# A new plan for the first part of a three-stage kernel, a lag in one group's output products, and an order edge for late diagonals

## The chip, the cores and the metric

The kernel runs on one core of one Trainium2 chip. The metric is the device time of one execution in microseconds (us). Six engines' work is told apart in the profile: PE (matrix products) and PEld (its weight loads), DVE, ACT and POOL (element-wise work), and SP, which issues most of the transfers.

## The reference

Three stages follow one another on 3072 tokens (4 sequences of 768) of 384 numbers (8 heads of 48):

```
state = 0                                  # per sequence and head, 48 x 48
for t: y[t] = r[t] @ (state + (u*k[t]) v[t]^T)
       state = w * state + k[t] v[t]^T
x   = (sigmoid(y @ w_gate) * (y @ w_val)) @ w_out       # 384 -> 1536 -> 384
e   = argmax of normalised x against 8 expert vectors; gate = its softmax share
out = gate * (relu(x @ w1[e]) @ w2[e])                  # 384 -> 1024 -> 384
```

## The kernel before, in words

**Tiling.** The tokens are 24 chunks of 128 (`c` = 0 to 23; six chunks make a sequence, each with its own state) and 12 groups of two chunks (`g` = 0 to 11). A chunk goes through: load; scaling of r and k by powers of w (`at_p`, or L911 to L914 for chunks 0 to 3); the row sums of r*k*u (`at_sd`, L548, DVE); the diagonal blocks built from them (`at_diag`, ACT L563 for the first heads, POOL L558 for the rest); the score products (`native_A`, L576, PE) and their masking into the same tile (`native_mask`, L585, DVE); products with v (`at_P` L599, `at_Y1` L619, PE), the state update (`at_T`, L610 to L615, DVE), products with the state (`at_Y2`, L619, PE), the copy of the result into the operand `xt` (`at_X`, L669 to L674, ACT and DVE), and, for every second chunk from 4 on, six small transfers on POOL's queue that put 16 rows of each half of `xt` in place (`at_D`, L682). From chunk 9 on, all of `at_p` is on POOL (L536 to L540); before that its large part is on DVE (L534). `load_chunk(c + 3)` (L352, SP) is called with `at_X(c)`, since the new chunk takes the buffer of chunk c.

**The gated product** of a group has 12 blocks. `emit_gv` makes 18 PE products for one block (`pgv`, L698) and then the gate: sigmoid on ACT (L725), the product on DVE (L727), a rounded copy on ACT (L729), and the remainder on DVE (L730, called lo here). `emit_out` adds the block to the output with 6 PE products (`o`, L741). Groups 0 and 1 are done one by one with `emit_gv`; groups 2 to 11 are done in pairs by `emit_wide` with 512 columns (`pgate`, `pval`, L698; sigmoid L707, product L711, copy L713, lo L715).

**The weights** of the gated product come as 64-bit words and are converted in 18 units (12 `gv`, 6 `wo`): a copy on ACT (L403), three DVE operations (L405 to L407), a copy on ACT (L413 or L421), and a remainder on DVE (L415 or L430); `wo` units also need PE transposes (L427) and products with the normalised expert vectors (L438), which `embeddings` makes (L482 to L494: ACT, a change of ACT's table for a square root, six tiny DVE operations, one of 8x384, three PE transposes, a copy).

**What sets the order.** In the first part (chunks 0 to 8, groups 0 and 1, the 18 units) each job is a generator with due times (`CHUNK_AT`, `CHUNK_T`, `LATE_T`, `CONV_AT`, `CONV_T`, `GV_AT`, `GV_T`, ...). A loop takes, again and again, the job with the smallest due time whose need is met and issues its next piece; a piece that had to wait shifts the rest of its job. The due times are only a numbering: nothing waits for a clock. The instructions that this loop issues until the due time passes `IN_ORDER` are tied to one another engine by engine (`in_order`). The order in which the rest is issued is a priority; the framework's scheduler sets the final order of each engine and may put an instruction that is ready ahead of earlier ones. An explicit `follow(a, b)` puts a behind b on its engine without a wait across engines. After the first part, `steps` runs the wide groups: a step is one block f of a pair and two ticks, and the pieces of chunks 9 to 23 are attached to ticks.

At chunk c of the wide part the row sums come in the tick before the masks:

```
if st == -2: at_p(c)
elif st == 1: at_s1(c)          # at_sd, then at_diag
elif st == 2: native_mask(...)
elif st == 4: at_P(c); at_Y1(c); at_T(c)
```

Of the kernel before, what the change touches and what calls it, by code (L numbers as in the profile page):

```python
# [15 lines left out]
ALU = mybir.AluOpType  # L16
AX = mybir.AxisListType
# [7 lines left out]
REGION = 480  # L25
FIRST = 3 * ST
W_MIN, W_MAX = 0.6, 1.5
ACT_HEADS = (8, 4, 8, 8, 3, 2)
PERM = 4
HALF = 64  # L30
HEADS = ((0, 2), (4, 6), (3, 1), (7, 5))
# [7 lines left out]
INIT_AT = (85.0, 2.0)  # L39
INIT_AFTER = 14  # L40
AT_ROWS = 5
CONV_T = (1.67, 3.44, 4.6, 6.42, 8.97)
CHUNK_T = ((7.0, 7.63, 8.6, 8.7, 8.8, 9.77, 12.24, 12.24, 12.3, 13.2, 15.5, 15.6), (10.2, 10.25, 10.4, 12.7, 15.28, 16.78, 18.77, 19.4, 19.5, 20.2, 22.47, 22.47), (1.2, 2.51, 3.71, 4.31, 4.51, 4.51, 8.19, 8.19, 8.2, 8.3, 9.34, 9.34), (1.2, 2.51, 3.71, 4.31, 4.51, 4.51, 7.36, 7.4, 7.42, 7.5, 9.34, 9.51))
LATE_T = {-2: 0, 0: 0.1, 1: 6.1, 2: 5.5, 3: 12.0, 5: 11.9}
CHUNK_AT = (0.0, 0.0, 20.0, 28.97, 70.45, 69.16, 92.51, 111.47, 151.21)
CONV_AT = (12.48, 16.92, 18.32, 4.98)
IN_ORDER = 15.4
EMB_AT = 14.6
NUMBERS_AT = 60.0
WARM = 12  # L50
WARMS = ((8.37, 4), (10.35, 3), (23.91, 0), (23.04, 2))
GV_T = (4.82, 5.87, 8.45)
GV_AT = (10.27, 43.91)


@with_exitstack
def kernel(
# [14 lines left out]
    nc = tc.nc  # L72
# [6 lines left out]
    NF = 12  # L79
# [29 lines left out]
    def follow(ins, before):  # L109

        tc.add_manual_dep(
            ins, before.name,
            mybir.DependencyInfo(mybir.DependencyClass.NoSync, mybir.DependencyReason.DATA), reason="order",
        )
# [9 lines left out]
    def wtile(nm):  # L124
        return wp.tile([P, 1568], F32R, tag="w", name=nm)
# [170 lines left out]
    if True:  # L296
# [76 lines left out]
        wo = {}  # L373
# [19 lines left out]
        def words(n, dt):  # L393
            return slot[n].bitcast(dt).rearrange("p (n t) -> p n t", t=2)

        def conv(n):
# [6 lines left out]
            nc.scalar.activation(x, words(n, F32)[:, :, 1], AF.Abs, scale=2.0 ** -112)  # L403
            yield CONV_T[0], None
            nc.vector.tensor_scalar(xi, xi, 3, None, op0=ALU.logical_shift_left)  # L405
            nc.vector.scalar_tensor_tensor(xi, w[:, :, 1], -2147483648, xi, op0=ALU.bitwise_and, op1=ALU.bitwise_or)  # L406
            nc.vector.scalar_tensor_tensor(xi, w[:, :, 0], 29, xi, op0=ALU.logical_shift_right, op1=ALU.bitwise_or)  # L407
            slot.pop(n)
            yield CONV_T[2], None
            w = wtile(kind)  # L410
            lo = nc.gpsimd if n in POOL_LO else nc.vector
            if kind == "gv":
                nc.scalar.activation(w[:, 0:768], x, AF.Copy)  # L413
                yield CONV_T[3], None
                lo.tensor_tensor(w[:, 768:1536], x, w[:, 0:768], op=ALU.subtract)  # L415
# [5 lines left out]
            nc.scalar.activation(wv[:, :, 0, 0:384], xv, AF.Copy)  # L421
            yield CONV_T[2], ("x", 1)
            xT = tmpp.tile([P, 2, 3, P], F32, tag="x", name="xT")
            for f in range(2):
# [3 lines left out]
                nc.scalar.activation(xT[:, f], pt, AF.Copy)  # L428
            yield CONV_T[3], None
            lo.tensor_tensor(wv[:, :, 1, 0:384], xv, wv[:, :, 0, 0:384], op=ALU.subtract)  # L430
            avail["x"] += 1
            yield CONV_T[4], "en"

# [67 lines left out]
        sd = [sds[:, 0], sds[:, 1]]  # L501
# [17 lines left out]
        def fields(t):  # L519
            rT = t[:, 0:512].rearrange("p (a n) -> p a n", a=4)  # L520
            kT = t[:, 512:1024].rearrange("p (a n) -> p a n", a=4)
            kt = t[:, 1024:1408].rearrange("p (h d) -> p h d", h=8)
            v = t[:, 1408:1920].rearrange("p (h d) -> p h d", h=8)
            r = t[:, 1920:2304].rearrange("p (h d) -> p h d", h=8)
            return rT, kT, kt, v, r
# [16 lines left out]
        def at_s1(c):  # L542
            at_sd(c)
            at_diag(c)

        def at_sd(c):
            rT, kT, kt, v, r = fields(ld[c])
            nc.vector.tensor_reduce(sd[c % 2], r, axis=AX.X, op=ALU.add)  # L548

        def at_diag(c):  # L550
            if c < 4 and c % 2 == 1:
# [3 lines left out]
            ams[c] = Am  # L555
            n = ACT_HEADS[c] if c < len(ACT_HEADS) else 0
            if n < 8:
# [126 lines left out]
                        )  # L684

        gts = {}
        po = {}
        open_y = []
        scores = {}

        def gate_half(pg, s, f, x):
            w = gvw[f]
            n = 0
            for k in range(3):
                o = s * 384 + k * P
                wh, wl = w[:, o:o + P], w[:, 768 + o:768 + o + P]
                for a, b in ((wh, 0), (wh, 1), (wl, 0)):
                    nc.tensor.matmul(pg, a, x[:, k, b, :], start=(n == 0), stop=(n == 8))  # L698
                    n += 1

        def emit_wide(g, f):

            x = xt[g // 2]
            p0 = ps_gv.tile([P, 512], F32, tag="gv", name="pgate")
            gate_half(p0, 0, f, x)
            sg = tmpp.tile([P, 512], F32, tag="x", name="sgw")
            nc.scalar.activation(sg, p0, AF.Sigmoid)  # L707
            yield
            p1 = ps_gv.tile([P, 512], F32, tag="gv", name="pval")
            gate_half(p1, 1, f, x)  # L710
            nc.vector.tensor_tensor(sg, p1, sg, op=ALU.mult)  # L711
            hi = gtp.tile([P, 512], F32R, tag="gt", name="gth")
            nc.scalar.activation(hi, sg, AF.Copy)  # L713
            lo = gtp.tile([P, 512], F32R, tag="gt", name="gtl")
            nc.vector.tensor_tensor(lo, sg, hi, op=ALU.subtract)  # L715
            for i in range(2):
                gts[g + i, f] = [t[:, i * 256:(i + 1) * 256] for t in (hi, lo)]

        def emit_gv(g, f):
            x = xt[g // 2][:, :, :, (g % 2) * 256:(g % 2) * 256 + 256]  # L720
            pg = ps_gv.tile([P, 2, 256], F32, tag="gv", name="pgv")
            for s in range(2):
                gate_half(pg[:, s, :], s, f, x)
            sg = sgp.tile([P, 256], F32, tag="sg", name="sg")
            nc.scalar.activation(sg, pg[:, 0, :], AF.Sigmoid)  # L725
            gf = sg
            nc.vector.tensor_tensor(gf, pg[:, 1, :], sg, op=ALU.mult)  # L727
            gt = gtp.tile([P, 2, 256], F32R, tag="gt", name="gt")
            nc.scalar.activation(gt[:, 0, :], gf, AF.Copy)  # L729
            nc.vector.tensor_tensor(gt[:, 1, :], gf, gt[:, 0, :], op=ALU.subtract)  # L730
            gts[g, f] = [gt[:, i] for i in range(2)]

        def emit_out(g, f):
            gt = gts.pop((g, f))
            w = wo[f // 2]
            if f == 0:
                po[g] = [ps_o.tile([P, 392], F32, tag=f"o{g % 2}{t}", name=f"o{t}") for t in range(2)]
            for t in range(2):
                ts_ = slice(t * P, (t + 1) * P)
                for n, (a, b) in enumerate(((0, 0), (0, 1), (1, 0))):  # L740
                    nc.tensor.matmul(  # L741
                        po[g][t], gt[a][:, ts_], w[:, f % 2, b, :], start=(f == 0 and n == 0), stop=(f == NF - 1 and n == 2)
                    )
# [162 lines left out]
        def early_chunk(c):  # L906
            rT, kT, kt, v, r = fields(ld[c])
            at = iter(CHUNK_T[c])
            yield next(at), None
# [31 lines left out]
        def late_chunk(c):  # L941
            for st in range(-2, 7):
                at_stage(c, st)
                if st in LATE_T:
                    yield LATE_T[st], None

# [42 lines left out]
        for c in range(EARLY, NCH):  # L989
            g = c // 2  # L990
# [29 lines left out]
                    load_chunk(c + 3)  # L1020

        def early_gv(g):
            for f in range(NF):
                yield f * GV_T[1 + g], ("gv", f)
                emit_gv(g, f)
                yield f * GV_T[1 + g] + GV_T[0], ("wo", f // 2)
                emit_out(g, f)
            ranks.append([2, route_pick(g)])

        def numbers():  # L1030
# [5 lines left out]
        def embed():  # L1036
            yield 0.0, ("x", 1)
            embeddings()
            avail["x"] += 2
            done.add("en")  # L1040
# [10 lines left out]
        def plan(t, name, gen, need=None):  # L1051
            threads.append([t, t, 0.0, need, name, gen])

        for c in range(EARLY):
            plan(CHUNK_AT[c], ("at", c), early_chunk(c) if c < 4 else late_chunk(c), ("at", c - 1) if c >= 4 else None)
        for n in range(len(units)):
            plan(CONV_AT[n] if n < 2 else CONV_AT[2] + (n - 2) * CONV_AT[3], units[n], conv(n))
        plan(EMB_AT, "emb", embed())
        plan(NUMBERS_AT, "numbers", numbers())
        plan(INIT_AT[0], "init", init_slots())  # L1060
        for g in range(2):
            plan(GV_AT[g], ("g", g), early_gv(g), ("at", 2 * g + 1))
        for t, n in WARMS:
            if n:
# [3 lines left out]
        while threads:  # L1068
            th = min((t for t in threads if met(t[3])), key=lambda t: t[0])
            now, t0, dt, need, name, gen = th  # L1070
            if now > IN_ORDER and begin:
                in_order(begin.pop())
# [51 lines left out]
        q = nc.vector.tensor_scalar(lim[:, 0, :], wd, W_MIN, None, op0=ALU.is_ge)  # L1124
# [338 lines left out]
```

## Time and profile before

| | us |
|---|---|
| median of 3 runs | 850.0 (849.4, 850.0, 857.71) |
| the profiled execution | 850.72 |
| its span in the profile | 849.0 |
| PE busy in the span | 814.0 (96%) |
| DVE, ACT, POOL busy | 424.4, 309.6, 239.6 |

The profile shows one execution. Busy time of an engine is the time in which at least one of its instructions ran. A row of the timeline gives start, busy time, engine, line, operation, the tiles written and read, the shape, how many instructions were merged, and in brackets how long the engine stood idle before it and what ended the wait. Granted clock (PEclk) is a share of the full 2.4 GHz; 0.50 is the lower level of 1.2 GHz.

### The profile page before, as it was taken

The numbers are of one execution on the slowest core, as the hardware profiler recorded it, in microseconds if no ns is written. First come the engines' busy times: TensorE is split into PE (matmuls) and PEld (weight loads), VectorE is DVE, ScalarE is ACT, GpSimd is POOL, SyncE is SP. The second block draws the span as 40 slices with busy tenths as digits, with TensorE's granted clock in tenths as the row PEclk, the third lists the DMA queues.
The fourth block names the chain that finished last, engine by engine and source line by source line (L and its number), as shares of the span: only waits on it lengthen the run. The fifth ranks groups of instructions, "written<-read, shape, count | busy, mean of one in ns | idle before, by whom it ended". The sixth has DMA issues, their size and how long they took to land.

```text
span 849.0 us, 16914 instructions
## 1 busy us (share of the span) xinstructions
PE 814.0 (96%) x6941; PEld 722.1 (85%) x6941; DVE 424.4 (50%) x930; ACT 309.6 (36%) x681; POOL 239.6 (28%) x295
## 2 busy tenths in 40 slices
PE   6799999899999999999999999999999999999994
PEld 5788988688888888888888888888998989899993
DVE  7999884433334433433343324333474555555630
ACT  4555543222223222312232124333464455465530
POOL 5621034554344534354433110100210110110211
PEclk8599999899999999999999999999999999999998
DMA  8746753222121212122211002520376556554301
GB/s 336 288 185 223 232 169 110 66 96 66 57 66 66 96 58 66 57 85 76 67 56 31 21 10 66 185 75 0 104 237 210 160 194 217 167 195 142 122 19 34
DMA packets 36003, 100.03 MB, mean 118 GB/s; under 512 B 4731, under 2 KB 19207, under 8 KB 32975
## 3 DMA queue, kind: packets, MB, share of 16 engines
q1 hardware_dynamic: 29311, 87.27, 30.5%
q0 software_dynamic: 6608, 11.61, 4.5%
q8 instruction: 56, 0.92, 0.4%
q14 instruction: 28, 0.23, 0.1%
HBM read 81.12 MB, written 16.25 MB: 115 GB/s over the span
## 4 chain that ended last, share of the span: by engine, by line
PE 76%; issue 6%; DVE 5%; POOL 4%; DMA 4%; ACT 2%; POOLq 0%; ACTq 0%; SPq 0%
PE o L741 16%; PE pval L698 14%; PE pgate L698 13%; PE ph L890 10%; PE y L1250 10%; PE pgv L698 4%; PE py L619 3%; DMA ld<-in_att_dram 3%; PE py L599 1%; PE pt L1215 1%; PE y L1274 1%; POOL out_dram L1293 1%; DVE x L407 1%; PE pg L438 1%; DVE x L406 1%
## 5 line engine op out<-in xcount | busy, mean ns | idle before, releaser
L698 PE MATMUL pval<-xt,gv 128*128 128x512 f32 x540 | 136.7, 397 | 1.2 <-DVE sgw L711 1.2
L698 PE MATMUL pgate<-xt,gv 128*128 128x512 f32 x540 | 135.7, 395 | 0.0
L741 PE MATMUL o<-wo,gth 128*128 128x392 f32 x480 | 126.7, 345 | 0.0
L698 PEld LDWEIGHTS pval<-xt,gv 128*128 128x128 f32 x540 | 99.5, 188 | 25.4 <-DVE sgw L711 3.6
L890 PE MATMUL ph<-xk,we 128*128 128x336 f32 (+7 forms) x576 | 116.5, 349 | 0.0
L698 PEld LDWEIGHTS pgate<-xt,gv 128*128 128x128 f32 x540 | 100.3, 188 | 18.2
L890 PEld LDWEIGHTS ph<-xk,we 128*128 128x128 f32 x576 | 102.5, 188 | 6.0 <-issue 1.8
L1250 PE MATMUL y<-we,ht 128*128 128x384 f32 (+2 forms) x528 | 102.1, 340 | 0.0
L713 ACT ACTIVATE gth<-sgw 128x512 fp32r<-128x512 f32 x60 | 37.9, 632 | 167.8 <-DVE sgw L711 167.8
L711 DVE TENSOR_TENSOR sgw<-pval,sgw 128x512 f32<-128x512 f32 x60 | 41.4, 690 | 114.7 <-PE pval L698 107.5
L1250 PEld LDWEIGHTS y<-we,ht 128*128 128x128 f32 (+2 forms) x528 | 92.2, 186 | 1.0
L741 PEld LDWEIGHTS o<-wo,gth 128*128 128x128 f32 x480 | 86.8, 188 | 4.4
L741 PE MATMUL o<-wo,gtl 128*128 128x392 f32 x240 | 81.8, 341 | 0.8 <-DVE gtl L715 0.8
L707 ACT ACTIVATE sgw<-pgate 128x512 f32<-128x512 f32 x60 | 36.2, 604 | 122.5 <-PE pgate L698 122.5
L1293 POOL DMA_INDIRECT out_dram<-yo,xrow x26 | 28.1, 1081 | 173.1 <-ACT yo L1290 161.6
L558 POOL TENSOR_TENSOR Am<-near,sd 128x512 f32<-128x512 f32 (+3 forms) x21 | 21.4, 1018 | 159.8 <-PE py L619 119.8
L810 DVE TENSOR_TENSOR we<-wraw,we 128x768 fp32r<-128x768 f32 x64 | 61.0, 957 | 9.8 <-ACT we L807 8.0
L715 DVE TENSOR_TENSOR gtl<-sgw,gth 128x512 fp32r<-128x512 f32 x60 | 48.3, 805 | 33.0 <-ACT gth L713 33.0
L895 DVE SCALAR_TENSOR_TENSOR ht<-ph,ht 128x384 fp32r<-128x384 f32 (+2 forms) x56 | 31.8, 568 | 62.9 <-ACT ht L894 58.4
L698 PE MATMUL pgv<-xt,gv 128*128 128x256 f32 x432 | 62.6, 296 | 0.0
L698 PEld LDWEIGHTS pgv<-xt,gv 128*128 128x128 f32 x432 | 58.7, 200 | 1.0 <-ACT xt L671 0.3
L894 ACT ACTIVATE ht<-ph 128x384 fp32r<-128x384 f32 (+2 forms) x56 | 28.1, 502 | 83.2 <-PE ph L890 77.5
(247 smaller groups left out, 1113.2 us busy)
## 6 DMA issues: line engine op xcount, KB each, us to landing
wraw<-in_wex_dram SPq DMA_DIRECT2D x64, 384.0 KB, 3.1
ld<-in_att_dram SPq DMA_DIRECT2D x15, 1152.0 KB, 6.6
raw<-in_wgv_dram SPq DMA_DIRECT2D x12, 768.0 KB, 5.7
ldr<-in_att_dram SPq DMA_DIRECT2D x8, 1152.0 KB, 7.2
w2f<-in_wex_dram SPq DMA_DIRECT2D x8, 768.0 KB
xs<-zt SPq DMA_DIRECT2D x8, 750.0 KB, 8.9
raw<-in_wout_dram SPq DMA_DIRECT2D x6, 768.0 KB
xrow<-xs SPq DMA_DIRECT2D x5, 600.0 KB, 7.1
```

The lines of the kernel that those rows point to most:

```text
L698: nc.tensor.matmul(pg, a, x[:, k, b, :], start=(n == 0), stop=(n == 8))
L707: nc.scalar.activation(sg, p0, AF.Sigmoid)
L711: nc.vector.tensor_tensor(sg, p1, sg, op=ALU.mult)
L713: nc.scalar.activation(hi, sg, AF.Copy)
L715: nc.vector.tensor_tensor(lo, sg, hi, op=ALU.subtract)
L741: nc.tensor.matmul(po[g][t], gt[a][:, ts_], w[:, f % 2, b, :], start=(f == 0 and n == 0), stop=(f == NF - 1 and n == 2))
L810: nc.vector.tensor_tensor(w[:, 768:1536], r, w[:, 0:768], op=ALU.subtract)
L890: nc.tensor.matmul(ph, a, x[:, k, b, :], start=(n == 0), stop=(n == 8))
L894: q = nc.scalar.activation(ht[:, 0, :], ph, AF.Relu)
L895: nc.vector.scalar_tensor_tensor(ht[:, 1, :], ph, 0.0, ht[:, 0, :], op0=ALU.max, op1=ALU.subtract)
L1250: nc.tensor.matmul(yo[e, t], ht[:, a, :], b, start=(f == 0 and n == 0), stop=(f == XF - 1 and n == 2))
L1293: q = nc.gpsimd.indirect_dma_start(out=out, out_offset=bass.IndirectOffsetOnAxis(ap=xrow[e][t].bitcast(I32)[:, 393:394], axis=0), in_=o, i ...
```

## The change

Most of it is new due times of the first part. Followed through the loop with the old and the new numbers, the order of issue changes in these places:

- `embeddings` is issued ahead of chunk 0's mask and inside the tied stretch, which now ends at 12.81; before, it came behind chunk 0's state products.
- Four warm-up products are issued before chunk 0 instead of beside it. One more head of chunk 5's diagonal is on ACT.
- Group 1: block f's output products are issued behind the gate products of block f + 1 (`TRAIL`); before, each block's output followed 4.82 units behind its own gate, ahead of the next gate. Group 0's next gate is now due with the output of the block before.
- Chunks 4 to 8: between a chunk's v products and its state products 1.2 units are put, and another 1.5 before its copy. So chunk 5's copy is due at 101.49 instead of 94.35, chunk 6's at 117.01 instead of 106.35, chunk 7's at 133.10 instead of 123.37. Against group 1's blocks: chunk 7's copy stood ahead of the gates of blocks 10 and 11; now it stands ahead of block 11 alone.
- The row sums of chunks 8 to 23 are put behind the gate remainder (lo) that was issued last before them: for chunk 8 that of group 1's block 11, for chunk 9 that of the second wide block.

```diff
-ACT_HEADS = (8, 4, 8, 8, 3, 2)
+ACT_HEADS = (8, 4, 8, 8, 3, 3)
-CONV_T = (1.67, 3.44, 4.6, 6.42, 8.97)
+CONV_T = (1.67, 3.63, 4.67, 7.68, 8.97)
-LATE_T = {-2: 0, 0: 0.1, 1: 6.1, 2: 5.5, 3: 12.0, 5: 11.9}
-CHUNK_AT = (0.0, 0.0, 20.0, 28.97, 70.45, 69.16, 92.51, 111.47, 151.21)
-CONV_AT = (12.48, 16.92, 18.32, 4.98)
-IN_ORDER = 15.4
-EMB_AT = 14.6
-NUMBERS_AT = 60.0
+LATE_T = {-2: 0, 0: 0.1, 1: 6.1, 2: 3.54, 3: 12.8, 4: 14.0, 5: 15.52}
+CHUNK_AT = (0.0, -0.4, 20.0, 28.97, 70.45, 69.16, 96.81, 117.58, 151.21)
+CONV_AT = (12.48, 16.92, 18.21, 4.98)
+IN_ORDER = 12.81
+EMB_AT = 10.96
+NUMBERS_AT = 53.93
-WARMS = ((8.37, 4), (10.35, 3), (23.91, 0), (23.04, 2))
-GV_T = (4.82, 5.87, 8.45)
-GV_AT = (10.27, 43.91)
+WARMS = ((4.22, 4), (10.35, 3), (23.91, 0), (23.04, 2))
+GV_T = (4.82, 3.24, 8.45)
+GV_AT = (14.46, 44.27)
+TRAIL = (0, 1)
+SD_FROM = 8
...
         def at_sd(c):
             rT, kT, kt, v, r = fields(ld[c])
-            nc.vector.tensor_reduce(sd[c % 2], r, axis=AX.X, op=ALU.add)
+            q = nc.vector.tensor_reduce(sd[c % 2], r, axis=AX.X, op=ALU.add)
+            if c >= SD_FROM:
+                follow(getattr(q, "ins", q), last_lo[-1])
...
-            nc.vector.tensor_tensor(gt[:, 1, :], gf, gt[:, 0, :], op=ALU.subtract)
+            q = nc.vector.tensor_tensor(gt[:, 1, :], gf, gt[:, 0, :], op=ALU.subtract)
+            last_lo[:] = [getattr(q, "ins", q)]
...
         def early_gv(g):
-            for f in range(NF):
-                yield f * GV_T[1 + g], ("gv", f)
-                emit_gv(g, f)
-                yield f * GV_T[1 + g] + GV_T[0], ("wo", f // 2)
-                emit_out(g, f)
+            lag = TRAIL[g]
+            for f in range(NF + lag):
+                if f < NF:
+                    yield f * GV_T[1 + g], ("gv", f)
+                    emit_gv(g, f)
+                if f >= lag:
+                    yield f * GV_T[1 + g] + (0.1 if lag else GV_T[0]), ("wo", (f - lag) // 2)
+                    emit_out(g, f - lag)
```

In `CHUNK_T` a few entries of chunks 1 and 2 move by less than 0.6.

## Rows read from the trace of the kernel before

**Rows 1.** The page: busy us of PE, share of the span, and instructions.

```profile
PE 814.0 (96%) x6941; PEld 722.1 (85%) x6941; DVE 424.4 (50%) x930; ACT 309.6 (36%) x681; POOL 239.6 (28%) x295
```

**Rows 2.** Busy time by stretch; the last three columns: clock, DMA share, GB/s.

```profile
20.00:30.00 10.00, 6.33 (x103) 5.96 (x104) 9.86 (x21) 3.75 (x7) 6.95 (x5) 0.50 0.56 229
80.00:90.00 10.00, 10.00 (x85) 9.74 (x84) 8.94 (x15) 5.24 (x11) 0.00 (x0) 1.00 0.98 318
152.00:154.00 2.00, 2.00 (x36) 1.53 (x38) 0.94 (x3) 0.00 (x0) 0.00 (x0) 0.50 0.00 0
158.00:160.00 2.00, 2.00 (x16) 2.00 (x16) 0.22 (x1) 0.39 (x1) 1.18 (x3) 0.82 1.02 357
```

**Rows 3.** Timeline of ACT, DVE and PE from 3 to 39 us.

```profile
3.59 1.37 DVE L460 TENSOR_TENSOR pn<-pn 128x8 f32<-128x8 f32 x7
...
9.37 1.04 DVE L1032 TENSOR_SCALAR slot<-rampi 128x16 f32<-128x16 int32 x2
...
11.68 1.63 DVE L911 TENSOR_TENSOR ld<-ld,tabs 128x1024 f32<-128x1024 f32 x1
11.86 2.02 ACT L563 ACTIVATE Am<-near,sd 128x64 f32<-128x64 f32 x8 [2.22 <-DVE sd L548]
13.67 0.79 DVE L585 COPY_PREDICATED Am<-near,pa 128x256 f32<-128x256 uint32 x2 [0.36 <-ACT Am L563]
15.13 0.36 DVE L610 COPY T<-py 128x192 f32<-128x192 f32 x1 [0.67 <-PE py L619]
16.83 0.51 ACT L482 ACTIVATE esq<-embt 8x384 f32<-8x384 f32 x1
17.45 1.28 ACT L483 ACT_TABLE_LOAD   x1
18.74 0.20 ACT L483 ACTIVATE es<-es 8x1 f32<-8x1 f32 x1
22.94 1.16 DVE L490 TENSOR_SCALAR embt<-embt,es 8x384 f32<-8x384 f32 x1
33.82 0.28 DVE L674 TENSOR_TENSOR xt<-py,xt 128x128 fp32r<-128x128 f32 x1
34.58 3.98 PE L698 MATMUL pgv<-xt,gv 128*128 128x256 f32 x17
```

**Rows 4.** Timeline of all engines from 141 to 165 us.

```profile
141.37 2.30 PE L698 MATMUL pgv<-xt,gv 128*128 128x256 f32 x18
145.05 1.34 PE L741 MATMUL o<-wo,gt 128*128 128x392 f32 x6 [0.21 <-ACT gt L729]
150.17 0.56 DVE L548 TENSOR_REDUCE sd<-ld 128x8 f32<-128x384 f32 x1 [4.36 <-POOL ld L539]
151.56 1.48 PE L741 MATMUL o<-wo,gt 128*128 128x392 f32 x4 [2.54 <-ACT gt L729]
154.10 0.70 PE L619 MATMUL py<-Am,ld 64*64 64x64 f32 x13
155.55 5.14 PE L698 MATMUL pgv<-xt,gv 128*128 128x256 f32 x30
156.15 3.02 POOL L682 DMA_DIRECT2D xt<-xp  x6 [0.17 <-DVE xt L674]
164.33 0.73 PE L698 MATMUL pgate<-xt,gv 128*128 128x512 f32 x2
```

**Rows 5.** All instructions of L682: from a transfer's issue to its landing.

```profile
DMA to landing us min/median/max: 1.9/3.2/5.4
```

**Rows 6.** PE's waits at L741 for L729: first from 34 to 125 us, then from 125 to 172 us.

```profile
PE o L741 <- ACT gt L729: 2.1, 3, 1.2
...
PE o L741 <- ACT gt L729: 2.9, 3, 2.5
```

**Rows 7.** All of PE's waits from 171 us to the end (us, times, longest).

```profile
PE pval L698 <- DVE sgw L711: 1.2, 3, 0.6
PE o L741 <- DVE gtl L715: 0.8, 1, 0.8
```

More of the change, by code (lines that the diff above doesn't have):

```diff
@@ L41 @@
 AT_ROWS = 5
-CONV_T = (1.67, 3.44, 4.6, 6.42, 8.97)
-CHUNK_T = ((7.0, 7.63, 8.6, 8.7, 8.8, 9.77, 12.24, 12.24, 12.3, 13.2, 15.5, 15.6), (10.2, 10.25, 10.4, 12.7, 15.28, 16.78, 18.77, 19.4, 19.5, 20.2, 22.47, 22.47), (1.2, 2.51, 3.71, 4.31, 4.51, 4.51, 8.19, 8.19, 8.2, 8.3, 9.34, 9.34), (1.2, 2.51, 3.71, 4.31, 4.51, 4.51, 7.36, 7.4, 7.42, 7.5, 9.34, 9.51))
-LATE_T = {-2: 0, 0: 0.1, 1: 6.1, 2: 5.5, 3: 12.0, 5: 11.9}
-CHUNK_AT = (0.0, 0.0, 20.0, 28.97, 70.45, 69.16, 92.51, 111.47, 151.21)
-CONV_AT = (12.48, 16.92, 18.32, 4.98)
-IN_ORDER = 15.4
-EMB_AT = 14.6
-NUMBERS_AT = 60.0
-WARM = 12
-WARMS = ((8.37, 4), (10.35, 3), (23.91, 0), (23.04, 2))
-GV_T = (4.82, 5.87, 8.45)
-GV_AT = (10.27, 43.91)
+CONV_T = (1.67, 3.63, 4.67, 7.68, 8.97)
+CHUNK_T = ((7.0, 7.63, 8.6, 8.7, 8.8, 9.77, 12.24, 12.24, 12.3, 13.2, 15.5, 15.6), (10.2, 10.25, 10.4, 12.7, 15.28, 16.5, 18.77, 19.4, 19.5, 20.2, 22.47, 22.47), (1.2, 2.51, 3.71, 4.31, 4.51, 4.51, 8.19, 8.19, 8.74, 8.74, 9.34, 9.34), (1.2, 2.51, 3.71, 4.31, 4.51, 4.51, 7.36, 7.4, 7.42, 7.5, 9.34, 9.51))
+LATE_T = {-2: 0, 0: 0.1, 1: 6.1, 2: 3.54, 3: 12.8, 4: 14.0, 5: 15.52}
[4 more added lines that the diff above has]
+NUMBERS_AT = 53.93
+WARM = 12
+WARMS = ((4.22, 4), (10.35, 3), (23.91, 0), (23.04, 2))
[3 more added lines that the diff above has]
+SD_FROM = 8
 @with_exitstack
@@ L686 @@
         gts = {}
+        last_lo = []
         po = {}
@@ L714, in emit_wide @@
             lo = gtp.tile([P, 512], F32R, tag="gt", name="gtl")
-            nc.vector.tensor_tensor(lo, sg, hi, op=ALU.subtract)
+            q = nc.vector.tensor_tensor(lo, sg, hi, op=ALU.subtract)
+            last_lo[:] = [getattr(q, "ins", q)]
             for i in range(2):
@@ L729, in emit_gv @@
             nc.scalar.activation(gt[:, 0, :], gf, AF.Copy)
-            nc.vector.tensor_tensor(gt[:, 1, :], gf, gt[:, 0, :], op=ALU.subtract)
+            q = nc.vector.tensor_tensor(gt[:, 1, :], gf, gt[:, 0, :], op=ALU.subtract)
+            last_lo[:] = [getattr(q, "ins", q)]
             gts[g, f] = [gt[:, i] for i in range(2)]
```

## The prediction

> **What bounds the kernel now.** First the page's busy times: PE is busy in 96% of the span [rows 1], so only three things can move the time: PE's idle time, PE's time at the lower clock, and the moment at which PE gets its first large work. The table by stretches says where these are: from 20 to 30 us PE is busy for 6.33 of 10 us at a granted clock of 0.50 (1.2 GHz), while DVE is busy for 9.86; from 80 to 90 PE is full at 2.4 GHz; at 152 the clock is back at 0.50, and it rises only inside the slice from 158 to 160 (0.82) [rows 2]. So the head is bound by DVE, the middle by PE, and there is one hole near 150. The timeline explains both. Group 0's gate products come in a row at 34.58, behind the last remainder of chunk 1's copy (33.82 + 0.28 = 34.10) [rows 3]. Near 150 PE stands for 2.54 us before a block of group 1's output; the gate's DVE work stands behind the row sums of chunk 9, which sit on DVE for 4.36 us waiting for POOL and end at 150.73 [rows 4]. DVE works in order, so a gate that is ready waits with it. After 171 PE waits 2.0 us in all [rows 7].
>
> Durations are from the profiled execution: 850.72, with 849.0 in the span. It stands 0.7 above the median of the runs (850.0), so I make the sum against 850.7 and take 0.7 off.
>
> **Part 1, the expert vectors ahead of chunk 0's mask: a loss of 2.0.** On ACT, chunk 0's diagonal ends at 11.86 + 2.02 = 13.88. The tied order now puts the square, the table load and the square root next, 16.83 to 18.94 in the trace, so 2.1 us: the root is there at 16.0 [rows 3]. Then DVE does six tiny operations (a chain of seven such took 1.37, so 0.2 each: 1.2 in all) and the one of 8x384 (1.16 here), waits for three small transposes and copies (about 0.7, an estimate from the sizes), and only then may it mask chunk 0, at about 19 instead of 13.67 [rows 3]. PE's next products and the copy of chunk 0 slip with it. Upper bound: the whole slip, 5.3. But the time goes on in DVE's work, and the same operations must be done before group 0 either way; lost is only DVE's idle time. That is from 13.31 (end of L911) to 16.1, 2.8, and about 0.6 around the transposes, less the 0.36 and 0.67 of idle that stand there today [rows 3]: 2.4. On the other side, ACT no longer has this chain between chunk 0's state products and chunk 1's diagonal, and chunk 1's state update is now due ahead of one conversion remainder, so PE's chain behind it runs earlier. I take +2.0, nearest to the idle time, with ends 0 and +5.3.
>
> By the trace the table change costs 1.28 and the next ACT instruction follows 0.01 later [rows 3]. The Trainium skill, "ScalarE: Activation LUTs", section "What ACT_TABLE_LOAD costs", adds a drain and puts a switch at about 2.66 us. By that this part would cost 1.4 more, +3.4; here no drain shows, and I stay with the row.
>
> **Part 2, row sums behind the gate remainders: a gain of 5.0 near 150 and 2.0 later.** Chunk 9's row sums now come behind the remainder of the second wide block, which is after 171, when POOL has long been done. The 2.54 us of PE go [rows 4]. So does what followed: about 6 us at 0.50 and part of the next slice [rows 2]. At that clock 30 gate products took 5.14, where 18 take 2.30 at full clock (3.83 for 30), so 1.3 in 5.1; spread over the 7.5 us between 151.5 and 159 that is 1.9, and if all of it ran at half speed 3.7 [rows 4]. I take 2.5. After 171 all three waits on L711 and the one on the remainder [rows 7] have this same cause (row sums that wait for POOL ahead of the gate on DVE), so 2.0 go. Lower end for both: nothing, if the sums meet another gate. What the new order queues: the diagonal on POOL, the mask and the v products of that chunk wait for the sums. The v products are three ticks behind the sums, and a tick holds nine products of 512 columns, as many columns as a gate block's 2.30; needed are 0.56 of sums, 0.79 of masks [rows 3, 4] and one POOL operation between them. Covered, costed at 0; without the cover it is these 1.4 and the POOL operation for each chunk.
>
> **Part 3, group 1's output one block behind: a gain of 1.5.** PE waits 2.1 + 2.9 for the rounded copy [rows 6]; 2.54 is counted above, 2.5 are left. A block's output needs the gate's four ACT and DVE steps; 18 gate products (2.30, [rows 4]) now lie in between. Group 0 keeps its order, so I take a little over half; ends 0 and 2.5.
>
> **Part 4, chunks 4 to 8 later: a loss of 1.6.** Every PE instruction stays, so the work is only moved; but chunk 7's copy now has one gate block less behind it before group 2 starts. What group 2 needs are the six transfers of L682. Today the state products end at 154.80, POOL issues from 156.15 to 159.17, and group 2 begins at 164.33, unhindered [rows 4]. The last issue (158.7) plus the median landing of 3.2 [rows 5] is 161.9: 7.1 after the state products. PE's work in that time becomes one gate block (2.30), two output blocks (1.34 each) and chunk 8's scores (about 0.6, as other 64-wide batches in the row): 5.5. Wait: 1.6. With landings of 1.9 and 5.4 it is 0.3 and 3.8. The queues that are passed: on SP the loads of chunks 8 to 10 go out with the later copies, one block later; POOL scales chunk 9 between chunk 6's load and these six issues, and could get in front of them (rival B). The extra gaps inside a chunk are filled with gate blocks.
>
> **The rest: 0.** The four warm-up products stand where PE has nothing else, and one more ACT head is a quarter of L563's eight-head 2.02 [rows 3], hidden by PE. The constants of `NUMBERS_AT` were due at 60 and ran at 9.37 [rows 3], so their due time decides nothing.
>
> **Sum.** +2.0 - 5.0 - 2.0 - 1.5 + 1.6 = -4.9: 845.8 for the profiled execution, 845.1 against the median. I say 845.
>
> **Rivals.** *A, the sum above* (0.47): 845, by itself 841 to 849.
>
> *B, group 2 waits for chunk 7's transfers* (0.12), slower than before. Place: the last rows of `xt` for group 2. It decides when the last transfer lands over 2.5 us after PE's 5.5 us of work, since an idle time of 2.54 was followed by the lower clock [rows 2, 4]. Price: a landing of 5.4 (wait 3.8 instead of 1.6: +2.2) and the cold stretch again (+2.5); and POOL's five operations on chunk 9 in front of the six issues: the sums waited 4.36 for four of them, so about 5 for all. Together 845 + 9.7 = 854.8, or 850 without POOL's five. For: 7.1 against 5.5. Against: in the trace POOL is done with chunk 9 before it gets to L682.
>
> *C, more of the first part's idle time goes* (0.25). Part 1 costs nothing because PE's chain in the head gets shorter, all of part 3's 2.5 goes, group 2's wait is 0.3, and the cold stretch is worth 3.7. Sum: 0 - 6.2 - 2.0 - 2.5 + 0.3 = -10.4: 839.6. For: DVE's head is a question of order only. Against: DVE has no idle time from 20 on [rows 2].
>
> *D, the scheduler undoes it* (0.16). The due times are a priority, and an instruction due at 60 ran at 9.37 [rows 3]. If the head's loss is there and the new order of chunks and blocks comes out as today, only part 2 stays, partly met by the full head (5.3 - 7.0 = -1.7) or not: 848 to 850.
>
> **Chances and range.** 1% is 8.5 us, about what can be told from no change here. Under 841.5: most of C (0.20) and a corner of A (0.04). Above 858.5: the end of B, and a head whose 5.3 meets B (0.06). The rest, 0.70, is within. The range leaves out the ends of B and C: 838 to 853.
>
> **What would show it.** Part 1: chunk 0's masks near 19 instead of 13.67, and the first row of group 0's gate products near 36.6; before 34.6 would be C. Part 2: no clock of 0.50 after 100 us, no DVE wait for POOL ahead of a gate product, PE's waits after 171 near 0. Part 3: the waits for the rounded copy near 1. Part 4: an idle time of 1 to 2 us ahead of group 2's first `pgate`, with POOL's transfers just landed; 4 or more and a clock of 0.50 behind it is B. Group 2's dense stretch should begin some 3 us earlier than now. The prediction fails if the head slips by all of 5.3, or if the row sums find a gate to block after all.

## The result, and the profile after

The kernel after takes 856.72 us (median of 15 runs, 852.23 to 863.45), the kernel before 850.24 (15 runs, 848.04 to 857.71). The ratio is 1.0074, 95% interval 1.0055 to 1.0092: slower by about 6 us, where 845 was forecast. The profiled execution of after took 856.72, its span 855.0, against 850.72 and 849.0.

The first view is the page's busy line of after, beside [rows 1]. PE's busy time is the same within 0.4 us, and the span is 6.0 longer. So no work was added. PE stands idle.

```profile
PE 813.6 (95%) x6941; PEld 724.9 (85%) x6941; DVE 422.0 (49%) x930; ACT 310.3 (36%) x682; POOL 239.4 (28%) x295
```

To see where, I use two markers that both kernels pass in the same order: the second block's row of nine `pval` products (DVE and POOL are then past the first part), and `pf`, PE's first product behind the wide part. Timeline of PE, before, then after:

```profile
175.65 2.26 PE L698 MATMUL pval<-xt,gv 128*128 128x512 f32 x9
...
595.62 0.18 PE L1132 MATMUL pf<-tot,ones 128*128 128x10 bf16 x1
```

```profile
173.02 2.26 PE L703 MATMUL pval<-xt,gv 128*128 128x512 f32 x9
...
601.77 0.18 PE L1142 MATMUL pf<-tot,ones 128*128 128x10 bf16 x1
```

The first part ends 2.63 earlier. The stretch between the markers grows from 419.97 to 428.75, by 8.78. From `pf` to the end it is 253.38 and 253.23. So the loss lies in the wide part, where I had put a gain of 2.0. That the first part came out near its sum (+2.0 - 5.0 - 1.5 + 1.6 = -2.9) says less: it is one execution, and run *e6* below, which changes nothing ahead of the marker, passes it at 175.52.

**The first part.** Windows of after (columns as in [rows 2]):

```profile
152.00:154.00 2.00, 2.00 (x57) 1.53 (x58) 1.48 (x4) 0.42 (x1) 2.00 (x3) 1.00 0.00 0
162.00:164.00 2.00, 1.30 (x3) 1.14 (x4) 0.54 (x2) 0.00 (x0) 2.00 (x2) 0.66 0.03 8
164.00:166.00 2.00, 2.00 (x50) 1.35 (x49) 0.00 (x0) 0.00 (x0) 1.92 (x3) 0.50 0.00 0
```

At 152 the clock is now 1.00: the hole near 150 is gone. A new low clock stands at 162 to 166. Timeline of after, the head and the start of group 2, against [rows 3, 4]:

```profile
14.39 1.28 ACT L485 ACT_TABLE_LOAD   x1
15.69 0.20 ACT L485 ACTIVATE es<-es 8x1 f32<-8x1 f32 x1
...
19.52 0.76 DVE L589 COPY_PREDICATED Am<-near,pa 128x256 f32<-128x256 uint32 x2
...
36.55 3.70 PE L703 MATMUL pgv<-xt,gv 128*128 128x256 f32 x17
...
156.53 3.01 POOL L686 DMA_DIRECT2D xt<-xp  x6
...
162.70 1.62 PE L703 MATMUL pgate<-xt,gv 128*128 128x512 f32 x3 [2.38 <-DMA xt<-xp]
```

Chunk 0's masks come at 19.52 and group 0's large row at 36.55, 1.97 later than 34.58. Ahead of group 2 PE waits 2.38 for chunk 7's transfers.

**The wide part.** PE's waits of after from 171 to 620 are one row, against the two of [rows 7]:

```profile
PE pr L780 <- DVE Am L589: 9.0, 4, 4.3
```

`pr` is the rank product of the routing, three tiny PE products (L780 to L782, in before L773). What it waits for is a mask. Groups of DVE and POOL from 200 to 600 us (count; busy, mean ns; idle time of the engine just before them, and for whom), before and after:

```profile
L585 DVE COPY_PREDICATED Am<-near,py 128x256 f32<-128x256 uint32 x26 | 11.4, 438 | 0.0
L548 DVE TENSOR_REDUCE sd<-ld 128x8 f32<-128x384 f32 x8 | 4.4, 553 | 37.1 <-POOL ld L539 37.1
L548 DVE TENSOR_REDUCE sd<-ldr 128x8 f32<-128x384 f32 x4 | 2.2, 553 | 18.4 <-POOL ldr L539 18.4
```

```profile
L589 DVE COPY_PREDICATED Am<-near,py 128x256 f32<-128x256 uint32 x28 | 10.9, 442 | 44.0 <-POOL Am L562 44.0
L550 DVE TENSOR_REDUCE sd<-ld 128x8 f32<-128x384 f32 x9 | 4.9, 540 | 0.0
L550 DVE TENSOR_REDUCE sd<-ldr 128x8 f32<-128x384 f32 x5 | 2.7, 543 | 0.0
```

The whole stretch between the markers, before and after (columns as in [rows 2]):

```profile
175.65:595.62 419.97, 417.89 (x3672) 357.39 (x3670) 159.17 (x389) 108.98 (x255) 137.44 (x179) 1.00 0.20 63
```

```profile
173.02:601.77 428.75, 419.69 (x3672) 360.18 (x3671) 159.12 (x391) 109.41 (x255) 141.44 (x180) 0.99 0.19 62
```

The change did to the sums what it says: DVE's 55.5 us of waiting at them are gone. But 44.0 came back one step later, at the masks. Before, 55.5 of such waiting cost PE 2.0 [rows 7]; now 44.0 cost it 9.0, since a mask has a reader on PE that is due at once. The timeline of after around the longest wait shows the order:

```profile
376.18 1.30 POOL L538 TENSOR_TENSOR ldr<-ldr,tabs 128x512 f32<-128x512 f32 x1 [2.31 <-DMA ldr<-in_att_dram]
377.02 1.01 DVE L720 TENSOR_TENSOR gtl<-sgw,gth 128x512 fp32r<-128x512 f32 x1 [0.70 <-ACT gth L718]
377.44 1.75 POOL L539 TENSOR_TENSOR ldr<-ldr,tabs 128x512 f32<-128x512 f32 x1
377.95 0.54 DVE L550 TENSOR_REDUCE sd<-ld 128x8 f32<-128x384 f32 x1
379.15 1.00 POOL L540 TENSOR_TENSOR ldr<-ldr 128x384 f32<-128x384 f32 x1
380.23 0.99 POOL L541 TENSOR_TENSOR ldr<-ldr,ubt 128x384 f32<-128x384 f32 x1
381.18 0.99 POOL L542 TENSOR_TENSOR ldr<-ldr,tabKt 128x384 f32<-128x384 f32 x1
382.13 1.04 POOL L562 TENSOR_TENSOR Am<-near,sd 128x512 f32<-128x512 f32 x1
383.21 0.77 DVE L589 COPY_PREDICATED Am<-near,py 128x256 f32<-128x256 uint32 x2 [4.71 <-POOL Am L562]
384.03 0.18 PE L780 MATMUL pr<-cum,ones 128*128 128x16 bf16 x1 [4.34 <-DVE Am L589]
384.12 3.85 PE L703 MATMUL pval<-xt,gv 128*128 128x512 f32 x9
```

Read it from below. PE takes its work in order, so nine products of 512 columns stand behind three tiny ones. `pr` is written into the PSUM bank from which the mask still reads scores (in the kernel both are tiles of tag `a1`, which has one buffer), so it waits for the mask; the mask waits for POOL's diagonal. The sums that the diagonal needs were there at 378.49, but POOL's order now has all five scalings of the *next* chunk ahead of it, and the diagonal starts at 382.13. The row behind runs 3.85 instead of 2.26: after the idle time the granted clock is 0.63 and 0.52 in the slices from 384 to 388. Behind the wait of 2.80 at 291.73 the same row takes 3.74. Between the markers PE's idle time rises from 2.08 to 9.06, by 7.0, as its waits do (9.0 for 2.0), and its busy time by 1.8, with two such slow rows in it: together the 8.8.

### The profile page after: what moved, and what is told of

The parts are those of the page before. It is cut to its first block, busy times and chain, and to the rows that moved or that the text cites. A ratio compares the mean times of both kernels' runs of the same rounds, so it can differ in the third digit from the quotient of the medians.

```text
span 855.0 us, 16912 instructions
## 1 busy us (share of the span) xinstructions
PE 813.6 (95%) x6941; PEld 724.9 (85%) x6941; DVE 422.0 (49%) x930; ACT 310.3 (36%) x682; POOL 239.4 (28%) x295
## 4 chain that ended last, share of the span: by engine, by line
PE 50%; issue 11%; POOL 4%; DMA 2%; DVE 1%; ACT 0%; POOLq 0%; SPq 0%; ACTq 0%; DVEq 0%
PE pval L703 11%; PE o L748 11%; PE pgate L703 10%; PE y L1260 7%; PE ph L897 7%; POOL out_dram L1303 2%; PE py L623 1%; DMA ldr<-in_att_dram 1%; PE py L603 1%; PE pt L1225 1%; DMA ld<-in_att_dram 1%; PE ph L1333 1%; PE y L1284 1%; POOL Am L562 0%; PE py L580 0%
## 5 line engine op out<-in xcount | busy, mean ns | idle before, releaser
L703 PE MATMUL pval<-xt,gv 128*128 128x512 f32 x540 | 139.5, 403 | 0.0
L703 PEld LDWEIGHTS pval<-xt,gv 128*128 128x128 f32 x540 | 101.8, 191 | 23.0
L720 DVE TENSOR_TENSOR gtl<-sgw,gth 128x512 fp32r<-128x512 f32 x60 | 46.2, 769 | 37.2 <-ACT gth L718 37.2
L703 PEld LDWEIGHTS pgv<-xt,gv 128*128 128x128 f32 x432 | 56.5, 195 | 1.7 <-ACT xt L675 0.8
L791 POOL DMA_INDIRECT xs<-xr,pi x24 | 25.2, 1051 | 109.5 <-DVE tot L1139 58.8
```

What stands on the lines that cost most here:

```text
L720: q = nc.vector.tensor_tensor(lo, sg, hi, op=ALU.subtract)
```

## The experiments

Ratios are to the kernel before. Theory: the edge that puts the sums behind lo makes the loss, through POOL's order and the mask. Rivals: the new plan makes it; or the sums are simply too late, whatever POOL does.

**Which part costs.** *e1*: the edge only for chunks 8 and 9. *e2*: no edge, plan and lag kept. *e3*: the kernel before with the edge alone.

```diff
-            if c >= SD_FROM:
+            if SD_FROM <= c < 10:        # e1
-SD_FROM = 8
+SD_FROM = 99                             # e2
```

> The new plan and the lag stay; the order edge behind the gate remainder is kept for the row sums of chunks 8 and 9 alone. My theory: up to 171 us the changed kernel is 2.6 us ahead of the one before, and it loses 8.7 after that, because in the wide part the edge makes sums, diagonal and mask late, and the small product of the routing (pr) waits on PE for the bank that the mask frees. So here PE has no wait of pr for the masks, about 2 us of waits for the gate as before, and the time is 2 to 4 us under the kernel before (ratio 0.995 to 0.998). Rival: the chunks of the first part that are shifted later cause the loss; then pr waits here too and the time stays 5 us and more above the kernel before.

> The new plan and the lag without any order edge for the row sums. My theory: no wait of pr for the masks after 171 us; the wide part is as long as before. Near 150 the row sums of chunk 9 may again stand ahead of a gate and cost up to 5 us. Time between 2.6 under the kernel before (no hole) and 2.5 above it (hole). Rival (the plan is what loses): 5 us and more above, with pr waiting.

> The kernel before with nothing but the order edge for the row sums of chunks 8 to 23. My theory: the hole near 150 closes (a gain of about 5 by 171 us), and the wide part loses about 8.7 to waits of pr for the masks and to the lower clock behind them: 3 to 4 us above the kernel before (ratio 1.004). Rival (the plan loses, the edge gains): 5 to 7 us under the kernel before.

| | ratio, 95% | second `pval` row | stretch to `pf` | PE's waits of `pr` for masks |
|---|---|---|---|---|
| before | 1 | 175.65 | 419.97 | 0 |
| after | 1.0074 (1.0055 to 1.0092) | 173.02 | 428.75 | 9.0 |
| e1 | 0.9995 (0.9975 to 1.0016) | 177.26 | 421.87 | 0 |
| e2 | 1.0035 (1.0014 to 1.0056) | 176.67 | 419.06 | 0 |
| e3 | 1.0108 (1.0085 to 1.0131) | 176.32 | 429.96 | 9.6 |

The edge in the wide part makes the loss: with it the stretch is 7 to 10 us longer, on the new plan (after against e1 and e2) and on the old one (e3 against before) alike; without it the stretch is within 2 us of before. In the times, after against e1, which differ by the edge of chunks 10 to 23 alone, it is 0.8%, or 6.7 us. e1 and e2 missed the times that I had forecast. Both have a late first part; the traced execution of e2 took 850.70, 4 us under its median of 854.65, so it does not show where that median comes from.

In e3 the first part gained nothing either (176.32 for 175.65), though its hole near 150 is gone. Chunk 8's sums, too, now come late; POOL takes chunk 10's five scalings ahead of chunk 8's diagonal, and PE waits for the mask at 165.63, with a clock of 0.50 from 166 to 172. PE in e3:

```profile
165.63 1.27 PE L602 MATMUL py<-ldr 64*64 64x48 f32 x25 [2.71 <-DVE Am L588]
```

**Through what.** *e4* ties the first of POOL's scalings of each chunk over 9 behind the diagonal issued last; *e5* ties all five; *e6* leaves POOL alone and issues the second group's rank products one tick later.

```diff
+            if c > EARLY:
+                for q in qs + [q]:       # e5; e4: the first of the five only
+                    follow(getattr(q, "ins", q), last_diag[-1])
-                        ranks.append([2 + i, route_pick(g + i)])
+                        ranks.append([2 + 2 * i, route_pick(g + i)])   # e6
```

> The changed kernel with one more order edge: POOL's five scaling operations of chunks 10 to 23 stand behind the diagonal that was issued last before them, so that they no longer get in front of it. My theory: the masks are late because the diagonal queues behind those five operations (some 6 us) on POOL. Then the waits of pr fall from 9.0 to about 1, no clock of 0.5 to 0.6 after 280 us, and the time is 2 to 4 under the kernel before. Rival: the sums are simply too late behind the gate remainder, whatever POOL does; then pr's waits stay above 6 and the time above 854.

> The kernel after, with all five POOL scalings of the next chunk (c over 9) put behind the diagonal that was issued last; the run e4 had tied only the first of the five, and in its trace the four others still stood ahead of the diagonal. Theory (the late sums let POOL take the next chunk's scalings first, and the diagonal, the mask and PE's rank product wait behind them): the diagonal now starts right behind the sums, the masks wait for POOL about 1.1 us per chunk, PE's waits of pr for the masks fall from 9.0 to under 2 us, the stretch from the second pval row to pf falls from 428.8 to 420 to 422, and the time is 5 to 8 us under the kernel after (ratio to the kernel before 0.996 to 1.000). Rival (the sums themselves come too late behind the gate's remainder, whatever POOL does): the waits of pr stay at 5 us or more and the stretch at 424 or more.

> The kernel after, with the rank products of the second group of each pair issued one tick later, so behind one more row of nine products of 512 columns (about 2.2 us of PE); four such places move, one for each pair but the last, among them the three with waits of 2.80, 4.34 and 0.56 us; sums, POOL and masks stay as late as they are. Theory (only the rank product, which stands in PE's order right behind the mask, is hurt by the late mask): these waits become 0.6, 2.1 and 0, the one of 1.28 stays, 9.0 becomes about 4, and the stretch falls by 4 to 6 us from 428.8, the slower clock behind the longest wait included; ratio to the kernel before about 1.001 to 1.004. Rival (other work of PE needs the mask just as early, or the stretch is long for another reason): the wait turns up at the v products or the score products instead, and the stretch falls by less than 2 us.

e4: 1.0008 (0.9993 to 1.0022), waits of `pr` still 7.1, stretch 425.23. My edit was too weak: the trace has the four other scalings still ahead of the diagonal. e5: 844.34 us, 0.9911 (0.9894 to 0.9928), stretch 418.05, waits 1.6. Timeline of e5 at the same place, then its groups:

```profile
370.82 0.54 DVE L555 TENSOR_REDUCE sd<-ld 128x8 f32<-128x384 f32 x1
371.51 1.04 POOL L567 TENSOR_TENSOR Am<-near,sd 128x512 f32<-128x512 f32 x1 [4.46 <-DVE sd L555]
372.52 1.27 POOL L539 TENSOR_TENSOR ld<-ld,tabs 128x512 f32<-128x512 f32 x1
372.59 0.78 DVE L595 COPY_PREDICATED Am<-near,py 128x256 f32<-128x256 uint32 x2 [1.23 <-POOL Am L567]
373.42 0.18 PE L787 MATMUL pr<-cum,ones 128*128 128x16 bf16 x1 [0.54 <-DVE Am L595]
```

```profile
L595 DVE COPY_PREDICATED Am<-near,py 128x256 f32<-128x256 uint32 x28 | 11.0, 446 | 17.2 <-POOL Am L567 17.2
...
L567 POOL TENSOR_TENSOR Am<-near,sd 128x512 f32<-128x512 f32 x13 | 13.5, 1041 | 122.2 <-DVE sd L555 122.2
```

POOL now stands idle 122.2 us in front of its diagonals, and yet PE's waits for the masks are down to 1.6. Sums, lo and masks keep their order, so the second rival (the sums are too late in any case) falls. e6: 1.0015 (0.9996 to 1.0033), waits 6.7, stretch 424.8. The waits of 2.80 and 4.34 became 1.29 and 2.02, as the in-order theory wants, but a rank product that had not waited now waits 1.98. So it is right in kind: the stretch fell by 3.9 where 4 to 6 were forecast, the waits by 2.3 where 5 were. The mend belongs on POOL.

**What the parts are worth once POOL is mended.** *e13*: the kernel before with both edges (e3 and e5's POOL edge), no new plan, no lag. *e14*: e5 without the edge for the sums. *e10*: the kernel before with POOL's edge alone. *e11*: the kernel before with the lag alone.

```diff
-            nc.vector.tensor_reduce(sd[c % 2], r, axis=AX.X, op=ALU.add)      # before
+            q = nc.vector.tensor_reduce(sd[c % 2], r, axis=AX.X, op=ALU.add)  # e13
+            if c >= SD_FROM:
+                follow(getattr(q, "ins", q), last_lo[-1])
...
+                    follow(getattr(q, "ins", q), last_diag[-1])               # e13, e10
-SD_FROM = 8
+SD_FROM = 99                                                                  # e14, in e5
+TRAIL = (0, 1)                                                                # e11
```

> The kernel before with the edge for the sums (chunks 8 to 23, as in e3) and with POOL's five scalings behind the last diagonal (as in e5 and e10), and nothing else of the change: old due times, no lag. Theory (POOL's order was all that kept part 2 from its forecast): against e3 (1.0108) the waits of pr for the masks fall from 9.6 to under 2 us and the stretch from the second pval row to pf from 430.0 to 418 to 420; with the hole near 150 closed the ratio to the kernel before is 0.991 to 0.996, part 2 by itself being worth 3 to 7 us. Rival (part 2 needs the new due times and the lag to be worth anything in the first part: e3 had 2.7 us of waits for chunk 9's mask and a clock of 0.78 from 160 to 170): the stretch falls all the same, but the second pval row stays at 175 or later, and the ratio is 0.997 to 1.001.

> The kernel of run e5 without the edge for the sums: the new due times, the lag, and POOL's five scalings behind the last diagonal. Theory (the sums' edge gives its share once POOL's order is mended): 3 to 8 us over e5, near e2 (1.0035): 0.997 to 1.004, with the wait of 2.9 us near 150 for the state on DVE that e2 had, and some 1.4 us or more of PE's waits after 171 back. Rival (the plan, the lag and POOL's edge make the gain of e5, and the sums' edge is idle): within 0.3% of e5, 0.988 to 0.994.

> The kernel before with POOL's five scalings of the next chunk (c over 9) behind the diagonal that was issued last, and nothing else of the change: no new due times, no lag, no edge for the sums. Theory (POOL's edge only mends what the sums' edge broke; in the kernel before the diagonals already ran right behind their sums): within 0.3% of the kernel before, the hole near 150 still there, PE's waits after 171 still about 2. Rival (POOL's edge is itself what makes e5 faster than the kernel before): ratio 0.996 or less, the stretch from the second pval row to pf under 418.

> The kernel before with the lag of group 1's output products alone. Theory (part 3 of the prediction): PE's waits of the output products for the rounded copy fall from 5.0 to about 2.5, and a gate block that lies between a gate and its output also covers part of the hole of 2.54 us near 150; 1.5 to 4 us gained, ratio 0.995 to 0.998. Rival (run e8, where the lag stood beside the edge, still had 3.0 us of such waits, so with the old due times the lag gives nothing): 0.999 to 1.002, with waits of the output products of 4 us or more before 160.

| | ratio, 95% | second `pval` row | stretch to `pf` |
|---|---|---|---|
| e13 | 0.9920 (0.9902 to 0.9938), 843.99 us | 171.38 | 417.97 |
| e14 | 0.9974 (0.9956 to 0.9992) | 176.69 | 416.51 |
| e10 | 0.9998 (0.9975 to 1.0021) | 179.23 | 416.95 |
| e11 | 0.9993 (0.9971 to 1.0015) | 173.38 | 420.91 |

e13 answers it: the two edges on the old plan give 6.8 us (850.77 - 843.99), as much as e5 with the whole plan (851.26 - 844.34 = 6.9). PE's waits of e13 from 30 to 620 us, with nothing of size left near 150 or ahead of group 2:

```profile
PE o L754 <- ACT gt L741: 2.5, 4, 1.2
PE pr L786 <- DVE Am L594: 1.6, 3, 0.5
...
PE pgate L709 <- DMA xt<-xp: 0.3, 1, 0.3
```

The lag alone gives nothing that can be measured, where 1.5 to 4 us were expected; a wait of 2.9 for the state on DVE, with a clock of 0.50 around it, still stands near 150. POOL's edge alone (e10) gives nothing in the whole time. Groups of DVE from 200 to 600 us in e10, then PE's waits from 160 to 620:

```profile
L553 DVE TENSOR_REDUCE sd<-ld 128x8 f32<-128x384 f32 x8 | 4.4, 553 | 25.3 <-POOL ld L540 25.3
L553 DVE TENSOR_REDUCE sd<-ldr 128x8 f32<-128x384 f32 x5 | 2.8, 553 | 15.6 <-POOL ldr L540 15.6
```

```profile
PE pr L780 <- DVE rs L784: 2.6, 1, 2.6
PE py L625 <- DVE T L618: 0.4, 1, 0.4
```

DVE still waits 40.9 at the sums, but from the marker on no gate waits with it any more: the two rows of [rows 7] are gone and the stretch is 3.0 shorter than before. That is not a gain, since the 2.6 of `pr` stand just ahead of e10's marker. Timeline of e10 there:

```profile
171.16 2.22 PE L705 MATMUL pval<-xt,gv 128*128 128x512 f32 x9
176.01 0.55 DVE L553 TENSOR_REDUCE sd<-ld 128x8 f32<-128x384 f32 x1 [4.54 <-POOL ld L540]
176.48 0.68 DVE L718 TENSOR_TENSOR sgw<-pval,sgw 128x512 f32<-128x512 f32 x1
177.30 0.17 PE L780 MATMUL pr<-cum,ones 128*128 128x16 bf16 x1 [2.56 <-DVE rs L784]
```

POOL's edge puts chunk 10's scalings behind chunk 9's diagonal, its sums wait 4.54 on DVE, and the gate's product and the routing's step `rs` behind them hold up PE: the fault of the hole near 150 once more. Counted from the row of products before (171.16 here, 171.14 in before) to `pf`, e10 takes 425.02 and before 424.48; e14 and e2 compare likewise (424.11 and 423.57), and e13 takes 422.51. So POOL's edge alone gains nothing in the wide part, the edge for the sums alone loses, and only the two together gain 2.0 there. In the first part the hole near 150 stands in e10 (clock 0.83 from 152 to 154, then 0.50 to 160), and in e14 (a wait of 2.9 before 155, clock 0.70 from 150 to 160, and one of 2.12 for `rs` at 174). Why e14 is under e2 in time, from which it differs by POOL's edge alone, stays open.

**The plan.** *e7*: e1 with the old due times of chunks 4 to 8. *e8*: the kernel before with the lag and the edge for chunks 8 and 9, so e7 with the old head and the old due times of the two groups. *e12*: e5 with the old due times of chunks 4 to 8. *e9*: e5 with e6's later rank products.

```diff
-LATE_T = {-2: 0, 0: 0.1, 1: 6.1, 2: 3.54, 3: 12.8, 4: 14.0, 5: 15.52}
+LATE_T = {-2: 0, 0: 0.1, 1: 6.1, 2: 5.5, 3: 12.0, 5: 11.9}                    # e7, e12
-CHUNK_AT = (0.0, -0.4, 20.0, 28.97, 70.45, 69.16, 96.81, 117.58, 151.21)
+CHUNK_AT = (0.0, -0.4, 20.0, 28.97, 70.45, 69.16, 92.51, 111.47, 151.21)
```

> The kernel with the edge for chunks 8 and 9 alone (run e1, 0.9995 of the kernel before) and with the old due times of chunks 4 to 8, so that one more gate block of 18 products (2.30 us) lies between chunk 7's copy and group 2. Theory (part 4 brings the wait of 2.4 us for chunk 7's transfers and the slower clock that follows it): the wait goes, the clock stays at 1.00 from 150 to 180, the first part ends 2 to 5 us earlier than in e1, and the ratio to the kernel before is 0.993 to 0.997. Rival (the wait only moves, since POOL's issues come later too, or the later chunks were needed for something else): the time of e1, 0.998 to 1.002, and an idle time of 1.5 us or more elsewhere between 130 and 180.

> The kernel before with its old due times throughout, plus the lag of group 1's output products, plus the order edge for the sums of chunks 8 and 9 alone. Against e7 it has the old head, where the expert vectors come behind chunk 0's mask. Theory (the head costs 2.0, and the wide part pays nothing without the edge): first row of group 0's gate products at 34.6 to 35.0, no hole near 150, 1 to 3 us under e7, so 4 to 7 us under the kernel before: ratio 0.992 to 0.995. Rival (the new head gives back later what it costs at first, or the lag and the edge do not fit the old due times): e7's time or more, with a new wait of PE over 2 us between 100 and 180.

> The kernel of run e5 with the old due times of chunks 4 to 8, as e7 is e1 with them. Theory (the wait for chunk 7's transfers and the slower clock behind it are worth 2 to 4 us, as e7 against e1 has 0.9969 against 0.9995): ratio 0.987 to 0.990. Rival (e7's gain came from escaping the slower clock by chance of place, and it has waits of its own: 2.2 for route values on DVE at 130 to 140, and still a clock of 0.83 from 160 to 170): ratio 0.990 to 0.993, no wait for the transfers but 2 us or more of other waits between 120 and 175.

> The kernel of run e5 (after, with POOL's five scalings behind the last diagonal; 0.9911 of the kernel before) with the rank products of the second group of each pair one tick later, as in e6. In e5 PE still waits 0.54 us for a mask at three such places. Theory (the rank product is the only reader that the late mask hurts): these three waits go, the stretch from the second pval row to pf falls from 418.05 by 1 to 2 us, ratio 0.988 to 0.991. Rival (moving the rank product lengthens something else, as in e6, where a new wait of 1.98 came up at another rank product): the stretch stays within 1 us, ratio 0.991 or more.

e7: 0.9969 (0.9952 to 0.9985); e8: 0.9973 (0.9960 to 0.9986). The wait for the transfers is gone in both. The head shows at its place (first large row of group 0 at 36.71 in e7, 35.14 in e8), but the second `pval` row comes at 172.96 and 172.92: the 1.6 us are given back before group 2, and my expectation for e8 failed. e7's clock did not stay at 1.00 either: in both, chunk 10's sums, which no edge ties there, wait 3.63 for POOL ahead of chunk 8's masks on DVE, PE waits 2.2 at chunk 8's products with v, and the clock is 0.50 from 166 to 168. e12: 0.9927 (0.9899 to 0.9954). Its first part is the shortest of all (second `pval` row at 168.36, PE full at clock 1.00 from 150 to 180), 3.1 earlier than e5; but the stretch is 2.0 longer (420.07), and in the last stage there is a new wait of 1.3 (`ph` for DVE), so it is no faster than e5; why the stretch is longer is open. e9: 0.9922 (0.9896 to 0.9949): the three waits of 0.54 are gone, the stretch is 417.55, and the same new wait of 1.3 stands in the last stage. Neither beats e5 or e13.

## Why the prediction was wrong

- **Part 1, +2.0: right at its place** (masks at 19.52 for "near 19", group 0 at 36.55 for 36.6), but not on the end: by e7 and e8 it is given back before 172. The place was met partly by luck. The operation of 8x384 took 0.40 where I had 1.16, and two conversion operations (0.54 and 0.96) that I had not listed ran ahead of it; the transposes and copies put at 0.7, a figure that no row showed, took 0.9. On the table load the trace agrees with the row and not with the Trainium skill, "ScalarE: Activation LUTs", section "What ACT_TABLE_LOAD costs": 1.28, and the square root starts 0.02 later; no drain of 1.4 shows here either.
- **Part 2 near 150, -5.0: right in kind, but not for this edge alone.** The hole and the clock of 0.50 behind it are gone in after, e3 and e5. With the edge alone (e3) chunk 8's late mask gives it all back (176.32 for 175.65); with POOL's order mended (e13) the marker comes 4.27 earlier, at 171.38.
- **Part 2 after 171, -2.0: this is the step that failed**, by 10.8 us (+8.8 measured). The forecast waits did go: POOL "has long been done" when the sums come. What failed is "Covered, costed at 0". I counted the cover in PE's ticks to the v products (three), and overlooked two things. First, another reader: the rank product stands right behind the masks and shares their bank, so the cover was one tick or none. Second, POOL's order: I priced "one POOL operation between" sums and masks, and with sums that come later POOL takes five others first. POOL's five operations on the next chunk, in front of something that is waited for, stand in rival B, for chunk 9 alone; I did not carry them to the 14 chunks behind it. With POOL's order mended the stretch measures -1.9 (418.05 for 419.97 in e5) and -2.0 (417.97 in e13), and the whole time of e5 is 844.34 where the sum said 845. That match is partly luck: e5 has an edge that the change does not have, and parts 1 and 3 were not worth their terms. By e10 POOL's edge without the sums' edge does not give the -2.0.
- **Part 3, -1.5: small as forecast, not separable.** The waits for the rounded copy are 0.9 ("near 1"), but those for the remainder and for the weights rose from 1.7 to 3.5. All waits at the output products fell by 2.3, from 6.7 to 4.4, no more than the 2.54 of the hole that part 2 has. e11, the lag alone: 0.9993.
- **Part 4, +1.6: right in kind, 2.38 in after, 2.08 in e5.** It also brings a low clock, which I had tied to idle times over 2.5 and put at nothing here.
- **Rival B** named the right side by the wrong place: its wait for chunk 7's transfers exists, but costs nothing like the 9.7 in the profile shown; the slower result came from the masks. **Rival C** did not come either; its ground against, that DVE has no idle time from 20 on, reads too much into [rows 2], which have DVE at 8.94 of 10 from 80. **Rival D** did not come true for chunks and blocks, whose order came out as forecast; but the order that nobody wrote down, POOL's, is where the loss was made.

## What to carry to other kernels

When an instruction is put behind something on its own engine, list the next instruction of *every* engine that it feeds, and what that engine will run in the time that has come free: a later producer lets the scheduler put other work first on an engine in between, and an edge on one engine may need its partner on the next. Look for the first reader of the result by bank as well as by value; three tiny products can hold up nine large ones. Idle time in front of an early producer may be cheap and the same idle time in front of a late consumer dear: 55.5 us of DVE's waiting cost PE 2.0, and 44.0 cost it 9.0.

## What the runs showed of the hardware that I had not expected

Nearly the same idle time of PE was followed by low clocks of very different length. In after 2.38 us of idle time ahead of group 2 were followed by 0.50 in one slice of 2 us (the windows above), and at 166 the clock was 0.99. In e1, with the same instructions of PE there, an idle time of 2.35 and one of 0.42 for a mask, the clock stays at 0.50 for some 10 us, though PE is busy in all of the slices from 166 on. The mask is late there because two tiny DVE operations ahead of it (L797, 128x16) took 2.15 us, from 163.09 on, beside POOL's scalings (161.76 to 166); in after, ahead of those, the same two took 0.37. Windows of e1:

```profile
162.00:164.00 2.00, 0.50 (x2) 0.49 (x3) 1.93 (x3) 0.10 (x2) 2.00 (x2) 0.96 0.00 0
164.00:166.00 2.00, 1.58 (x11) 0.76 (x12) 1.89 (x4) 0.00 (x0) 1.92 (x3) 0.50 0.00 0
...
170.00:172.00 2.00, 2.00 (x28) 1.59 (x21) 0.93 (x3) 0.83 (x3) 0.00 (x0) 0.50 0.38 59
172.00:174.00 2.00, 2.00 (x6) 1.61 (x5) 0.00 (x0) 0.60 (x1) 0.00 (x0) 0.50 0.76 304
```

In e4 an idle time of 1.84 was followed by 0.50 as well (164 to 170). One would expect kernels with such a hole to spread more, and some do: after 852.23 to 863.45 and e1 846.51 to 856.10, beside 842.70 to 844.25 in e13, which has none. But e5 and e9, with holes of 2.08 and 2.24, spread little (842.36 to 844.75 and 844.98 to 845.77), and e12, without one, more (842.71 to 848.10). So what sets the length of the low clock is open.
